# Attention with a mixture of experts on one core: where TensorE turns the inner layer of a tile, and which tests stand around it

## The chip, the core and the metric

The kernel runs on one core of a Trainium2 chip, as one launch. The metric is device time in microseconds (us). Three runs of the kernel before took 515.75 to 516.62 us, with a median of 516.23 us. Five engines work side by side, each with its own queue of instructions: TensorE (PE in the profile; its weight loads are listed apart as PEld), VectorE (DVE), ScalarE (ACT), GpSimd (POOL) and SyncE (SP, which starts most transfers). They wait for each other through semaphores: counters that an instruction raises when it is done, and on which another engine waits for a number.

## The reference

What is computed is causal attention followed by a mixture of experts in which every token goes to one expert:

```python
# q, k, v: (4, 12, 448, 64)
scores = q @ k^T / 8, masked above the diagonal
x = softmax(scores) @ v, laid out as (1792 tokens, 768)
# 8 experts, w1: (8, 768, 1024), w2: (8, 1024, 768)
logits = (x / |x|) @ (emb / |emb|)^T / tau
expert_idx = argmax(logits); gate_w = softmax(logits)[expert_idx]
for e in range(8):
    h = maximum(x[mask] @ w1[e], 0)
    out[mask] = gate_w[mask] * (h @ w2[e])
```

## The kernel before, in words

The first 220 us or so are the attention, whose order is written out by hand in a table; the change does not touch it. Then come the experts. Tokens are sorted by expert on the chip and cut into tiles of up to 128 tokens, each of one expert. With the inputs of the runs there are 18 tiles, numbered t = 0 to 17. Expert 4, the one with most tokens, comes first (tiles 0 to 4); the others follow in the order of their numbers.

Each tile has two matrix products. The first (`product1`, 768 to 1024) runs over 6 blocks of 128 rows of w1; its sums are copied to a tile `hb[t]`, the inner layer. The inner layer must be turned (transposed) before the second product (`product2`, 1024 to 768), which runs over 8 blocks of 128 rows of w2. To keep precision, numbers are split into a high and a low part (h and l): a block takes 6 matmuls (high by high, high by low, low by high, for two halves of the width). ACT casts the high part of a weight and DVE subtracts to get the low part; this is `split_w`, done only where a tile's expert is new.

Three kinds of tiles are told apart by a number that is computed on the chip and read into a register of each engine (`few[t]`):

- 1, a small tile: at most 64 tokens. High and low lie side by side in one operand, and a block takes 4 matmuls.
- 2, a light tile: over 64 tokens, and of the same expert as the tile before, so that no weights have to be split. Its inner layer is turned by DVE (16 transposes of 32 columns, `turn_light`), and TensorE turns nothing.
- 0: over 64 tokens, and of a new expert. TensorE turns the inner layer with 8 transposes (`turn_h`).

Tiles 2, 3, 7, 10, 13, 14 and 15 are light, tiles 4, 5, 8 and 17 are small, and tiles 6, 9, 11, 12 and 16 are neither. Tile 1 is treated as a whole tile without a test. A new expert begins at tiles 5, 6, 9, 11, 12, 16 and 17.

The loop `body(t)` writes out the work of the tile in flight. On TensorE the order is: first product of tile t, turn of the input rows of tile t+1 (`turn_x`), the first 7 blocks of the second product of tile t-1, the turn of the inner layer of tile t, and the last block of the second product of tile t-1. On ACT and DVE it is: split w1 for tile t+1 if its expert is new, copy the inner layer of tile t (`hiddens`), split the input of tile t+1 (`next_x`), DVE's turn if tile t is light, split the first 6 blocks of w2 for tile t if its expert is new, split the turned inner layer (`split_h`), scale and store tile t-1 (`finish`), split the last two blocks of w2. After the last tile there is no further first product: `last` runs its second product and stores it.

Since the tiles' kinds are known only on the chip, each choice is a test and a jump in every engine's queue (`either` and `branch`). All arms of such a choice must raise an engine's semaphore by the same amount by the place where they meet, so an arm in which an engine has nothing to do gets one instruction that waits for the engine's own earlier work and then raises the count (on TensorE line 577 of the helper `branch`). From tile 14 on the body stands inside a test on the number of tiles (`rest`, line 974), whose other arm, with the call of `last`, lies far behind in the program.

Of the kernel before, what the change touches and what calls it, by code (L numbers as in the profile page):

```python
# [16 lines left out]
ET = mybir.EngineType  # L17

P = 128
# [106 lines left out]
def attn_moe(tc, qk, vv, emb, tau, w1, w2, out):  # L126
# [3 lines left out]
    with ExitStack() as ctx:  # L130
# [10 lines left out]
        def cut(a, parts, *dims, at=0):  # L141

            n = 1
            for d in dims:
                n *= d
            a = a[:parts, at : at + n]
            if len(dims) == 1:
                return a
            names = "abcd"[: len(dims)]
            return a.rearrange(f"p ({' '.join(names)}) -> p {' '.join(names)}", **dict(zip(names, dims)))  # L150
# [3 lines left out]
        sp_ring, pt_ring = Ring(bank[0:2], bank[2:4]), Ring(*bank[4:6])  # L154
# [60 lines left out]
        def part(tile_, i, j, *dims):  # L215

            def f():
                t, n = tile_(), 1
                for d in dims:
                    n *= d  # L220
                return cut(t, P, *dims, at=i * DM + (j or 0) * F)
            return f
# [8 lines left out]
        th_ring = Ring(part(rr, 1, 0, KF, P), part(or_, 1, 0, KF, P))  # L231
        tl_ring = Ring(part(qr, 5, 0, KF, P), part(pr, 9, 0, KF, P))
# [325 lines left out]
        xs, hs, hb = {}, {}, {}  # L558
# [11 lines left out]
        def load_few(t, engines):  # L570
            return nc.values_load(small[0:1, t : t + 1], engines=engines, min_val=0, max_val=2,
                                  skip_runtime_bounds_check_because="made on chip within these bounds")

        def branch(flag, small_, whole_, light_=None):

            def rest():
                with tc.If(flag > 1) as c:
                    light_()
                with c.Else():
                    whole_()  # L580
            with tc.If(flag == 1) as c:
                small_()
            with c.Else():
                rest() if light_ else whole_()

        def either(t, engine, small_, whole_, light_=None):

            if t < 2:
                whole_()
            else:  # L590
                branch(few[t][engine], small_, whole_, light_)
# [21 lines left out]
        pf = {}  # L613

        def turn_x(t):
            xs[t] = (xs[t], xh_ring.next(), xl_ring.next())
            px = [cut(pt_ring.next(), P, 3, P) for a in range(2)]
            for a, pt in enumerate(px):
                for k in range(3):
                    pe.transpose(pt[:, k], xs[t][0][:, (3 * a + k) * P : (3 * a + k + 1) * P], idt)  # L620
            return px
# [2 lines left out]

        def turn_h(t):

            pf[t] = [cut(pt_ring.next(), P, 4, P) for a in range(2)]
            hs[t] = (hb[t], th_ring.next(), tl_ring.next())

            def rows(n):  # L630
                for k in range(KF):
                    pe.transpose(pf[t][k // 4][:, k % 4, 0:n], hb[t][0:n, k * P : k * P + P], idt[0:n, 0:n])
            either(t, ET.PE, lambda: rows(64), lambda: rows(P), lambda: None)

        def turn_light(t):

# [35 lines left out]
        def product(acc, xh, xl, wh, wl, ks, ends, w):  # L672

            for k in ks:
                for j in range(2):
                    o = slice(w * j, w * j + w)
                    pe.matmul(acc[j], xh[:, k], wh[k][:, o], start=k == ends[0], stop=False)  # L677
                    pe.matmul(acc[j], xh[:, k], wl[k][:, o], start=False, stop=False)  # L678
                    pe.matmul(acc[j], xl[:, k], wh[k][:, o], start=False, stop=k == ends[1])  # L679

        def small_product(acc, x, wh, wl, ks, nk, w):

            for k in ks:
                for j in range(2):
                    o = slice(w * j, w * j + w)
                    pe.matmul(acc[j], x[:, k], wh[k][:, o], start=k == 0, stop=False)
                    pe.matmul(acc[j], x[:, k], wl[k][:, o], start=False, stop=k == nk - 1)

        few = [None] * NT

        def product1(t, acc):
            either(t, ET.PE, lambda: small_product(acc, xs[t][1], h1, l1, range(KD), KD, 512),
                   lambda: product(acc, *xs[t][1:], h1, l1, range(KD), (0, KD - 1), 512))

        def product2(t, acc, ks=range(KF)):
            either(t, ET.PE, lambda: small_product(acc, hs[t][1], h2, l2, ks, KF, 384),
                   lambda: product(acc, *hs[t][1:], h2, l2, ks, (K0[0], K0[-1]) if t == 0 else (0, KF - 1), 384))

        def hidden(t, acc, j):
            if t not in hb:  # L700
                hs[t] = hb[t] = hh_ring.next()
            ac.copy(hb[t][:, 512 * j : 512 * j + 512], acc[j])  # L702

        def hiddens(t, acc):

            hs[t] = hb[t] = hh_ring.next()

            def low(j):
                return hb[t][0:64, 512 * j : 512 * j + 512]

            either(t, ET.Activation, lambda: [ac.copy(low(j), acc[j][64:128]) for j in range(2)],
                   lambda: [hidden(t, acc, j) for j in range(2)])
            either(t, ET.DVE, lambda: [v.tensor_tensor(low(j), acc[j][0:64], low(j), op=ALU.add) for j in range(2)],
                   lambda: v.memset(apart, 0.0))

        acc2 = [bo[:, :384], bx[:, :384]]
# [123 lines left out]
        pt_ring = Ring(*bank[2:6])  # L840
# [7 lines left out]
        def loads(t, which):  # L848
            if t >= NT:
                return  # L850
            if ee[t] is None:
                ee[t] = val(t, E - 1, [ET.SP])
                cc[t] = val(NT + t, 1, [ET.SP, ET.Activation, ET.DVE, ET.Pool])
            load(*((r1, w1, KD) if which == 1 else (r2, w2, KF)), ee[t], cc[t] != 0)

        def split_w(r, h, l, ks):
            for k in ks:
                ac.copy(h[k], r[:, k])  # L858
                v.tensor_tensor(l[k], r[:, k], h[k], op=ALU.subtract)  # L859

        def body(t):
            product1(t, acc1)
            if t == 1:
                halves()
            if t == 2:
                upper()
            elif t == 1:
                hidden(t, acc1, 0)
                hidden(t, acc1, 1)
            if t + 1 < NT:  # L870
                with tc.If(cc[t + 1] != 0):
                    split_w(r1, h1, l1, range(KD))
                loads(t + 2, 1)
            if t > 1:
                hiddens(t, acc1)
            if t + 1 < NT:
                few[t + 1] = {e: load_few(t + 1, [e]) for e in (ET.PE, ET.DVE, ET.Activation)}
            if t + 1 < NT:
                next_x(t + 1, turn_x(t + 1))
            if t + 3 < NT:  # L880
                gather(t + 3)
            if t == 1:
                gates()
            turn_light(t)
            ks = K0[GE:] if t == 1 else list(range(KF))
            product2(t - 1, acc2, ks[:-1])
            turn_h(t)
            product2(t - 1, acc2, ks[-1:])
            if t > 1:
                with tc.If(cc[t] != 0):  # L890
                    split_w(r2, h2, l2, range(6))
            split_h(t)
            finish(t - 1, acc2, False)
            if t > 1:
                with tc.If(cc[t] != 0):  # L895
                    split_w(r2, h2, l2, range(6, KF))
            loads(t + 1, 2)
# [35 lines left out]
        def halves():  # L933

            v.tensor_scalar(sm, us, 1.0 / SKIP, None, ALU.mult)
            f = pt_ring.next()[:, :NT]
            pe.matmul(f, idt[:, 64:65].broadcast_to([P, P]), sm, start=True, stop=True)
            same, t2 = T("same", [NT], parts=1), T("t2", [NT], parts=1)
            v.memset(same, 0.0)
            v.tensor_tensor(same[:, 1:], ef[:, 1:NT], ef[:, 0 : NT - 1], op=ALU.is_equal)  # L940
            v.tensor_tensor(t2, f[0:1], same, op=ALU.mult)
            v.tensor_tensor(same, same, t2, op=ALU.subtract)
            v.scalar_tensor_tensor(small, same, 2.0, f[0:1], op0=ALU.mult, op1=ALU.add)

        def upper():

            f = pt_ring.next()[:, :NT]
            pe.matmul(f[64:128], idt[:, 0:64], gt, start=True, stop=True, tile_position=(0, 64), skip_group_check=True)
            v.tensor_copy(gu[64:128], f[64:128])
# [67 lines left out]
```

## Time and profile before

| | |
|---|---|
| median of three runs | 516.23 us |
| the profiled execution | 516.48 us, of which the span of the instructions is 514.7 us |
| mean granted TensorE clock over the span | 0.992 |
| TensorE busy | 490.8 us (95% of the span) |
| VectorE busy | 348.4 us (68%) |
| ScalarE busy | 338.2 us (66%) |

The busy shares are means over attention and experts. The matmuls are pipelined, so that the time one is listed with (0.33 us) overlaps with the next: what counts is the distance between two starts, 0.17 us for a matmul of 384 columns. "PEq" is TensorE's sequencer, which reads the instructions, waits for semaphores and takes the jumps; it runs ahead of the matmuls.

### The profile page before, as it was taken

What the parts mean: (1) busy time and instruction counts of PE and PEld (TensorE: products, weight loads), DVE (VectorE), ACT (ScalarE), POOL (GpSimd) and SP (SyncE); (2) the same over time, 40 slices, a digit from 0 to 9 for tenths busy, and PEclk for the clock granted to TensorE, in tenths of its full rate; (3) what the DMA queues carried; (4) which work ended last, traced back from release to release, by engine and by line L of the source; (5) the groups of instructions that cost most, each with busy time, mean ns of one, the idle gap of its engine ahead of it and who ended that gap; (6) DMA issues with size and microseconds to landing.
All of it is one profiled execution on the core that took longest, in us unless ns stands there. A gap on an engine that the chain in (4) does not pass through costs nothing. (4 is left out here: it accounts for less than half of the span.)

```text
span 514.7 us, 10584 instructions
## 1 busy us (share of the span) xinstructions
PE 490.8 (95%) x3120; PEld 391.2 (76%) x3120; DVE 348.4 (68%) x945; ACT 338.2 (66%) x813; POOL 81.1 (16%) x90
## 2 busy tenths in 40 slices
PE   8999999999999978999999999999999999999983
PEld 5566566665666646889889898899989988898983
DVE  4776576586668659554486986846988454788871
ACT  5999999999999997231245963617566531256770
POOL 2000000000000560330111122200721020011101
PEclk9999999999999999899999999999999999999998
DMA  8223443263345960311349684368587312567831
GB/s 250 71 95 108 123 148 108 73 197 109 108 124 179 330 215 18 93 33 62 134 176 379 243 279 158 152 231 355 195 294 283 130 63 69 241 212 289 284 130 34
DMA packets 27368, 87.19 MB, mean 169 GB/s; under 512 B 2694, under 2 KB 3142, under 8 KB 27280
## 3 DMA queue, kind: packets, MB, share of 16 engines
q1 hardware_dynamic: 24160, 72.38, 40.8%
q0 software_dynamic: 3120, 13.77, 7.5%
q8 instruction: 39, 0.64, 0.5%
q14 instruction: 49, 0.40, 0.2%
HBM read 144.33 MB, written 12.58 MB: 305 GB/s over the span
## 5 line engine op out<-in xcount | busy, mean ns | idle before, releaser
L378 ACT ACTIVATE aq<-aq,mx 112x112 f32<-112x112 f32 (+3 forms) x192 | 99.8, 524 | 4.2 <-DVE mx L373 4.2
L373 DVE CUSTOM_DVE_ANT_0 aq<-bank,ar 112x112 f32<-112x112 f32 (+1 forms) x192 | 76.1, 442 | 30.0 <-PE bank L368 29.7
L396 PE MATMUL bank<-idt,aq 112*112 112x112 f32 x480 | 62.6, 265 | 1.6 <-ACT ap L401 0.8
L396 PEld LDWEIGHTS bank<-idt,aq 112*112 112x112 f32 x480 | 46.8, 133 | 19.8 <-ACT ap L401 7.0
L743 POOL DMA_INDIRECT out_dram<-fa,isx x18 | 32.5, 1803 | 179.4 <-DVEq L895 42.7
L368 PE MATMUL bank<-ak 64*112 64x112 f32 (+3 forms) x384 | 56.2, 416 | 0.9 <-DVE mx L373 0.8
L401 ACT COPY ap<-bank 112x336 f32<-112x336 f32 (+2 forms) x120 | 51.3, 459 | 2.9 <-PE bank L396 1.1
L409 PE MATMUL bank<-ap 112*64 112x448 f32 (+3 forms) x384 | 51.2, 406 | 1.1 <-ACT ap L401 1.1
L859 DVE TENSOR_TENSOR wl<-fa,wh 128x1024 fp32r<-128x1024 f32 x42 | 48.4, 1220 | 4.5 <-PE bank L678 2.7
L702 ACT COPY fa<-bank 128x512 f32<-128x512 f32 x28 | 15.2, 588 | 54.0 <-PE bank L677 49.3
L642 DVE STREAM_TRANSPOSE turned<-fa 32x256 f32<-32x256 f32 x112 | 48.8, 435 | 1.5
L409 PEld LDWEIGHTS bank<-ap 112*64 112x64 f32 x384 | 25.1, 136 | 31.6 <-issue 17.7
L858 ACT CAST wh<-fa 128x1024 fp32r<-128x1024 f32 x42 | 40.7, 1048 | 5.6 <-PE bank L679 3.1
L562 POOL DMA_INDIRECT fa<-xd,ig x21 | 24.0, 1144 | 84.8 <-PE bank L620 56.6
L378 ACT ACTIVATION_READ_ACCUMULATOR aq<-aq,mx 112x1 f32 x192 | 36.9, 192 | 0.0
L368 PEld LDWEIGHTS bank<-ak 64*112 64x112 f32 x384 | 27.0, 173 | 12.9 <-issue 3.1
L679 PE MATMUL bank<-wh,akr 128*128 128x512 f32 x84 | 32.9, 392 | 1.3 <-DVE akr L601 1.3
L677 PE MATMUL bank<-wh,aor 128*128 128x512 f32 x84 | 32.8, 391 | 0.2 <-ACT aor L600 0.2
L677 PE MATMUL bank<-wh,akr 128*128 128x512 f32 x84 | 33.0, 393 | 0.0
L679 PE MATMUL bank<-wh,apr 128*128 128x512 f32 x84 | 32.9, 392 | 0.0
L678 PE MATMUL bank<-wl,aor 128*128 128x512 f32 x84 | 32.8, 391 | 0.0
L678 PE MATMUL bank<-wl,akr 128*128 128x512 f32 x84 | 32.8, 390 | 0.0
(291 smaller groups left out, 1060.7 us busy)
## 6 DMA issues: line engine op xcount, KB each, us to landing
fa<-in_w_dram SPq DMA_DIRECT2D x76, 768.0 KB
fa<-in_w_dram SPq DMA_DIRECT2D x54, 1024.0 KB
ak<-in_qk_dram SPq DMA_DIRECT2D x24, 448.0 KB
ap<-in_vv_dram SPq DMA_DIRECT2D x24, 224.0 KB
xd<-fa SPq DMA_DIRECT2D x3, 1344.0 KB
fa<-in_w_dram SPq DMA_DIRECT2D x6, 512.0 KB
xd<-fa SPq DMA_DIRECT2D x1, 1120.0 KB
fa<-xd,ig POOLq DMA_INDIRECT x21, 5.7
```

Source lines behind the costliest of these rows:

```text
L368: pe.matmul(o, raws[p % 4][rows, 0, CP * i : CP * i + CP], raws[p % 4][rows, 1, :n], start=True, stop=True, tile_position=(D * h, 0), skip ...
L373: v.tensor_tensor_reduce(out=Ps[p % 2][i, h], in0=st.pop(("sp", p, i, h)), in1=mask[i], scale=-0.125, scalar=3e38, op0=ALU.add, op1=ALU.mi ...
L378: ac.activation(x, x, AF.Exp, bias=mxs[p % 3][:, h, i : i + 1], scale=-1.0, accum_out=sums[p % 3][:, h, i : i + 1])
L396: pe.transpose(t[:, x, c], Ps[p % 2][i, h][:, c * CP : c * CP + CP], idt[:CP, :CP])
L401: (ac.copy if q == "A" else v.tensor_copy)(o, st.pop(("pt", p, n)))
L409: pe.matmul(bo[64 * h : 64 * h + 64, CP * c : S], vts[p % 4][:, c, 64 * h : 64 * h + 64], PTs[p % 2][:, h, 4 * c : 3 * c + NC], start=c == ...
L642: v.transpose(xk[32 * j : 32 * j + 32, :, q : q + 32], blocks[q : q + 32, :, j])
L677: pe.matmul(acc[j], xh[:, k], wh[k][:, o], start=k == ends[0], stop=False)
L678: pe.matmul(acc[j], xh[:, k], wl[k][:, o], start=False, stop=False)
L679: pe.matmul(acc[j], xl[:, k], wh[k][:, o], start=False, stop=k == ends[1])
L858: ac.copy(h[k], r[:, k])
L859: v.tensor_tensor(l[k], r[:, k], h[k], op=ALU.subtract)
```

## The change

```diff
         def turn_h(t):
-            pf[t] = [cut(pt_ring.next(), P, 4, P) for a in range(2)]
-            hs[t] = (hb[t], th_ring.next(), tl_ring.next())
-
             def rows(n):
                 for k in range(KF):
                     pe.transpose(pf[t][k // 4][:, k % 4, 0:n], hb[t][0:n, k * P : k * P + P], idt[0:n, 0:n])
-            either(t, ET.PE, lambda: rows(64), lambda: rows(P), lambda: None)
+            either(t, ET.PE, lambda: rows(64), lambda: rows(P))
...
+        def turned_h(t, acc, ks):
+            pf[t] = [cut(pt_ring.next(), P, 4, P) for a in range(2)]
+            hs[t] = (hb[t], th_ring.next(), tl_ring.next())
+
+            n = 3 if t > 1 else 1
+
+            def among():
+                product2(t - 1, acc, ks[:-n])
+                turn_h(t)
+                product2(t - 1, acc, ks[-n:])
+            if t < 2:
+                among()
+            else:
+                with tc.If(few[t][ET.PE] > 1) as c:
+                    product2(t - 1, acc, ks)
+                with c.Else():
+                    among()
...
             ks = K0[GE:] if t == 1 else list(range(KF))
-            product2(t - 1, acc2, ks[:-1])
-            turn_h(t)
-            product2(t - 1, acc2, ks[-1:])
+            turned_h(t, acc2, ks)
```

Where tile t is light, TensorE now runs the whole second product of tile t-1 in one arm, with no test between its blocks. Where it is not, the product is cut after its fifth block instead of its seventh, and the turn stands there. The matmuls and transposes that are executed are the same ones. The program of TensorE gets longer, since the second product is written out in both arms.

TensorE's queue, second product of tile 3 around its last block (bank 72 and 73 are its two accumulators, 69 and 70 the turned layer; "waits PE_49" is a wait for TensorE's own count), before:

```order
L679 MATMUL bank_73<-apr 128x384
L581 UNCONDITIONAL_BRANCH
L871 UNCONDITIONAL_BRANCH
L581 UNCONDITIONAL_BRANCH x2
L581 COMPARE_AND_BRANCH
...
L581 UNCONDITIONAL_BRANCH
L577 COMPARE_AND_BRANCH
L577 UNCONDITIONAL_BRANCH [waits PE_49]
...
L581 COMPARE_AND_BRANCH
L686 MATMUL bank_72<-apr,aor 128x384 [waits Activation_49]
```

and after, the end of the light tile's arm (lines 674 to 676 are the former 677 to 679):

```order
L674 MATMUL bank_73<-apr,aor 128x384
L675 MATMUL bank_73<-apr,aor 128x384
L676 MATMUL bank_73<-apr 128x384
L674 MATMUL bank_72<-apr,aor 128x384 [waits Activation_49]
L675 MATMUL bank_72<-apr,aor 128x384 [waits DVE_49]
L676 MATMUL bank_72<-apr 128x384
L674 MATMUL bank_73<-apr,aor 128x384
L675 MATMUL bank_73<-apr,aor 128x384
L676 MATMUL bank_73<-apr 128x384
L581 UNCONDITIONAL_BRANCH
```

The seventh and the eighth block now follow each other, and the wait for TensorE's own count with its two tests is gone from between them; behind the arm stands one jump over the arm for the other tiles.

TensorE's queue in the other arm, after the fifth block of the same product (line 629 is the former 632, the transposes):

```order
L674 MATMUL bank_73<-apr,aor 128x384
L675 MATMUL bank_73<-apr,aor 128x384
L676 MATMUL bank_73<-apr 128x384
L581 UNCONDITIONAL_BRANCH
L581 COMPARE_AND_BRANCH
L629 MATMUL bank_69<-idt,fa 128x64 [waits DVE_49,Activation_49]
L629 MATMUL bank_69<-idt,fa 128x64 x3
L629 MATMUL bank_70<-idt,fa 128x64 [waits DVE_49,Activation_49]
L629 MATMUL bank_70<-idt,fa 128x64 x3
```

The transposes, which stood behind the seventh block, stand behind the fifth, with the same waits for DVE and ACT; three blocks of the product follow them.

## Rows read from the trace of the kernel before

**Rows 1.** The page: TensorE's busy time, and its granted clock in 40 slices.

```profile
PE 490.8 (95%) x3120; PEld 391.2 (76%) x3120; DVE 348.4 (68%) x945; ACT 338.2 (66%) x813; POOL 81.1 (16%) x90
PEclk9999999999999999899999999999999999999998
```

**Rows 2.** Waits of TensorE from 235 to 515 us: total, times, longest.

```profile
PE bank L677 <- PEq L577: 4.6, 7, 0.7
PE bank L686 <- DVE fa L735: 1.3, 1, 1.3
```

**Rows 3.** Line 577 from 235 to 515 us: duration ns min/median/max, first to last start.

```profile
L577 PEldq COMPARE_BRANCH  x19: 77/169/215, 242.5 to 479.5; - x19
L577 PEldq EVENT_SEMAPHORE  x7: 51/51/51, 245.6 to 464.3; - x7
```

**Rows 4.** Timeline, TensorE, light tile 10: start us, us, line, [idle before <-releaser].

```profile
372.77 0.33 PE L679 MATMUL bank<-apr 128*128 128x384 f32 x1
...
373.29 0.34 PE L679 MATMUL bank<-apr 128*128 128x384 f32 x1
374.32 0.44 PE L677 MATMUL bank<-apr,aor 128*128 128x384 f32 x1 [0.69 <-PEq L577]
374.61 0.34 PE L678 MATMUL bank<-apr,aor 128*128 128x384 f32 x1
```

**Rows 5.** Timeline, TensorE, light tile 2, the first.

```profile
245.18 0.34 PE L679 MATMUL bank<-apr 128*128 128x384 f32 x1
245.94 0.44 PE L677 MATMUL bank<-apr,aor 128*128 128x384 f32 x1 [0.42 <-PEq L577]
246.22 0.33 PE L678 MATMUL bank<-apr,aor 128*128 128x384 f32 x1
```

**Rows 6.** Timeline, TensorE, tile 11, whose inner layer TensorE turns.

```profile
391.47 0.34 PE L679 MATMUL bank<-apr,aqr 128*128 128x384 f32 x1
391.64 1.03 PE L632 MATMUL bank<-idt,fa 128*128 128x128 f32 x8
392.43 0.42 PE L677 MATMUL bank<-apr,arr 128*128 128x384 f32 x1
```

**Rows 7.** Timeline, TensorE, tile 5: its turn within the small tile 4.

```profile
291.46 0.34 PE L687 MATMUL bank<-apr,arr 128*128 128x384 f32 x1
291.73 0.71 PE L632 MATMUL bank<-idt,fa 64*128 64x64 f32 x8
```

**Rows 8.** Timeline, DVE: what those two turns wait for (tile 5, then tile 11).

```profile
289.50 1.27 DVE L713 TENSOR_TENSOR fa<-bank,fa 64x512 f32<-64x512 f32 x2
...
387.60 0.06 DVE L714 MEMSET apart<- 1x1 f32 x1
```

**Rows 9.** Busy time by stretch: us, then busy us of each engine.

```profile
235.00:375.00 140.00, 137.52 (x740) 123.97 (x739) 100.11 (x162) 71.11 (x108) 28.35 (x17) 1.00 0.60 220
```

**Rows 10.** Timeline, TensorE, second products of tiles 16 and 17.

```profile
490.29 0.42 PE L677 MATMUL bank<-arr 128*128 128x384 f32 x1
...
493.15 0.33 PE L678 MATMUL bank<-aqr,arr 128*128 128x384 f32 x1
...
499.40 0.34 PE L679 MATMUL bank<-apr,aqr 128*128 128x384 f32 x1
501.09 0.41 PE L686 MATMUL bank<-arr,aor 128*128 128x384 f32 x1 [1.35 <-DVE fa L735]
```

**Rows 11.** Timeline, ACT, the first cast of w2 for tile 17.

```profile
493.52 0.84 ACT L858 CAST arr<-fa 128x768 fp32r<-128x768 f32 x1 [1.75 <-PE bank L678]
```

**Rows 12.** Timeline, DVE: first low part of w2 and the turned layer of tile 17.

```profile
494.40 0.96 DVE L859 TENSOR_TENSOR aqr<-fa,arr 128x768 fp32r<-128x768 f32 x1 [2.23 <-ACT arr L858]
...
499.62 0.75 DVE L666 SCALAR_TENSOR_TENSOR aor<-bank,aor 128x256 fp32r<-128x256 f32 x2
```

**Rows 13.** Line 974 from 490 to 503 us: TensorE's jump to the last product.

```profile
L974 PEldq COMPARE_BRANCH  x1: 3797/3797/3797, 497.0 to 497.0; - x1
```

## The prediction

> **What bounds the kernel now.** [...] Then the waits of TensorE over the stretch of the experts. They come to two entries only: seven waits on its own sequencer, released at line 577, together 4.6 us, and one of 1.3 us before the very last product [rows 2]. Everything else in this stretch is matmuls end to end. So time is won by taking idle time out of TensorE's queue, and lost by putting some in; DVE and ACT matter where TensorE comes to wait for them.
>
> Line 577 is the arm of the light tiles in which TensorE has nothing to turn. It is taken seven times [rows 3], once for each light tile. The sequencer reads the test long before it matters: the first test is at 242.5 us, and the wait that follows it ends at 245.6 us [rows 3], so that the sequencer stands 3.1 us ahead of the matmuls. Then it waits there until TensorE's own matmuls are done, and loses its lead: in tile 10 the last matmul of the seventh block starts at 373.29 and the next one at 374.32 us [rows 4]. Where TensorE turns the layer itself, the same tests cost it nothing: matmul, transposes and matmul follow each other at 391.47, 391.64 and 392.43 us [rows 6].
>
> **The change part by part.**
>
> *The second product in one piece, seven times.* Matmuls of this product start 0.173 us apart (three steps from 372.77 to 373.29) [rows 4]. The first start after the gap is 1.03 us late instead of 0.173, and the one behind it comes 0.29 us after that instead of 0.173 (374.32 to 374.61): 0.97 us lost. The first light tile loses less, 0.76 and 0.28 instead of 0.173 each, so 0.69 us [rows 5]. The tests and the wait between the blocks go in the new arm, and no wait of another engine stood between these blocks to take their place. Gain: 6 x 0.97 + 0.69 = 6.5 us, all of it on the path, since TensorE is what bounds. One jump at the arm's end comes in; the sequencer's lead of 3.1 us hides it as it hides those around the transposes.
>
> *The test in the other tiles' body.* The test for a light tile moves from inside the turn to ahead of the product. Small tiles have one test more. At a median of 169 ns a test [rows 3] and with 3.1 us of lead: nothing. If the lead were gone, 4 x 0.17 us.
>
> *The turn two blocks earlier, in nine tiles (4, 5, 6, 8, 9, 11, 12, 16, 17).* The transposes are the same. They now need the inner layer 2 x 6 x 0.173 = 2.08 us earlier, or 2 x 4 x 0.173 = 1.39 us where the tile before is small. Two places come close. At tile 5 DVE's second half of the layer is done at 290.77 us [rows 8], and the transposes start at 291.73 [rows 7], their second half about 0.3 us later; 1.39 us earlier, that half would start at 290.64 and waits 0.1 to 0.2 us. If DVE did not follow the 1.66 us that tiles 2 and 3 have won by then, it would be 1.8 us. I take 0.15, as DVE adds up sums that come from TensorE and so moves with it. At tile 11 the turn waits for a memset by which DVE closes its branch (387.60 us [rows 8], the turn at 391.64 [rows 6]): 3.98 us of room. Off that go 2.08 for the earlier place, 1.73 for the late release described next (at tile 9, behind which DVE has a light tile's transposes and then weights to split), and 0.97 of tile 10, which DVE does not follow while it works without a break. That is 0.8 us too much at worst, nothing at best; I take 0.4. What the earlier turn gives ACT and DVE is nothing here: where the expert is new, both have six blocks of w2 to split ahead of the turned layer, and where it is not, `finish` still has to wait for the product's end.
>
> *A release that comes later.* This is not in the diff. A cast of a block of w2 for a new expert overwrites the block that the second product of the tile before reads; it waits for a count of TensorE. All arms must reach equal counts, and in the built program the count for the first cast is reached at the third matmul of the fifth block, where before it was the fifth matmul of the third: 10 matmuls or 1.73 us later (whole tile before; for a small one about as much or somewhat more). That this wait binds is seen at the end: matmul number 17 of the product that begins at 490.29 starts at 493.15 and runs 0.33 us [rows 10], and the cast starts at 493.52, released by that line [rows 11]. Six of the seven new experts have the first product of the next tile between this and the use of the weights, which hides it. Tile 17 has none: its second product comes right behind. DVE's chain there runs from the cast (493.52) over the first low part (494.40) and six of them to the turned layer at 499.62, of which the first half is done about 0.42 us later, at 500.04 [rows 11, 12]. Before, TensorE had to wait longer than that: until 501.09 [rows 10], because its sequencer was in the jump of line 974 from 497.0 for 3.80 us, that is until 500.8 [rows 13]. Counted from the product's start, DVE is now ready at 500.04 - 490.29 + 1.73 = 11.48 us, and the last product can start at some 11.6; before it started at 10.80. Cost 0.8 us. Bounds: 1.73, if the profile's releaser (DVE's scaling at line 735, which comes behind the turned layer) is the true one; -0.5, if DVE's chain doesn't move and the jump is read 0.5 us earlier (3.1 us ahead of the end instead of 499.57 - 497.0 = 2.6).
>
> *Sum.* -6.5 + 0.15 + 0.4 + 0.8 = -5.2 us against the profiled execution's 516.48 us: 511.3. The median of the runs shown is 0.25 us below that execution, so 511.0 us. With the costs at their least: -6.5 - 0.5, so 509.2; at their most (1.8, 0.8 and 1.73): -2.2, so 514.0.
>
> **The rivals.**
>
> *The skipped code has to be fetched (slower).* Every tile now jumps over an arm of up to 96 matmuls, where the largest arm skipped inside the body before had 36. The one long jump on the path took the sequencer 3.80 us [rows 13]. If every skip cost as much, it would exceed the lead of 3.1 us by 0.7 us in 16 bodies: 11 us, so 522 us. It decides from the point where a skip takes over 3.1 us. For it speaks that line 974 is the same kind of instruction; against it, that this jump goes past whole bodies of tiles and that each of the seven light arms and nine others skips far less than one body.
> [...]
>
> *The gain is handed back in waits (no change).* If DVE and ACT stand still in time instead of following TensorE, for instance because weights land no sooner, each turned tile waits for its layer: nine times 0.6 us and the tail's 1.73 use up the 6.5 us: 516 us. For it: tile 5 has under 1 us of room. Against: DVE is busy for 100.1 of 140 us in this stretch [rows 9], and no wait of TensorE for DVE, ACT or a transfer appears before the tail [rows 2].
>
> *The idle time moves instead of going (less faster).* If the sequencer doesn't get its lead back by the arm's end, the jump there costs part of what the wait cost; with half of it left, 3.3 us return: 514.3 us. Against it: the tests around the transposes, which come as thickly, cost nothing [rows 6].
>
> **How the numbers follow.** The forecast has a chance of 0.76, the fetched code 0.07, the handed-back gain 0.08, the idle time that moves 0.09. Differences of up to 0.2% (1.03 us) can't be told from no change in this kernel. So faster: 0.76 + 0.09 = 0.85; within 0.2%: 0.08; slower: 0.07. The range goes from 509.2, the least costs, to 514.3, which takes in the greatest costs and the third rival.
>
> **What would show it.** In the profile after, the seven waits for the sequencer are gone from TensorE's list, and starts in a light tile are 0.17 us apart through all eight blocks. Turns at tiles 5 and 11 show waits of under 1 us. The first cast of w2 for tile 17 comes about 5.0 us after the start of tile 16's second product, instead of 3.2, and the last product starts 11.6 us after it instead of 10.8. I am wrong if gaps stand in front of first products or turns (fetching), if TensorE waits for DVE in most turned tiles, or if the last product starts no later than before.

## The result: slower, and the profile after

The changed kernel takes 520.48 us (median of four runs, 520.44 to 521.60) against 515.99 us for the kernel before on the same chip (four runs, 515.67 to 516.62): a ratio of 1.0087, 95% interval 1.0075 to 1.0099. It is slower by 4.5 us, where 511.0 us was forecast. The range (509.2 to 514.3) doesn't hold the time, and the case that came true is the rival "the skipped code has to be fetched", which had a chance of 0.07. The ratios in this document leave out two executions that took far longer than the others of the same kernel: one of 2199 us in the first run of experiment 4, and one of 702 us of the kernel before.

The profiled execution has a span of 518.7 us, 4.0 more than before. First the page, the answer to [rows 1]:

```profile
PE 491.9 (95%) x3120; PEld 392.6 (76%) x3120; DVE 348.3 (67%) x945; ACT 337.8 (65%) x813; POOL 81.2 (16%) x90
PEclk9999999999999999999999999999999999999997
```

The instructions are the same in number. TensorE is busy for 1.1 us more than before and idle for 2.9 us more, so most of the 4.0 us are idle time; the other part is matmuls that took longer, and is read below. Its waits from 235 to 520 us (total, times, longest) answer to [rows 2]:

```profile
PE bank L675 <- issue: 2.8, 1, 2.8
PE bank L683 <- DVE aor L663: 2.2, 1, 2.2
PE bank L674 <- issue: 1.4, 2, 0.9
PE bank L674 <- DVE fa L730: 0.5, 1, 0.5
PE bank L674 <- DVE turned L639: 0.3, 1, 0.3
```

The seven waits for line 577 are gone. New are waits of lines 674 and 675 for "issue", which means that the profile shows nothing the engine waited for. Line 581 is a test on TensorE's sequencer (PEldq); its row over the experts (duration in ns min/median/max) has the same median as the kernel before's, 205, but that one's longest was 338:

```profile
L581 PEldq COMPARE_BRANCH  x69: 63/205/3800, 243.5 to 501.8; - x69
```

Now light tile 10, the answer to [rows 4], with what stands behind it:

```profile
372.18 0.33 PE L675 MATMUL bank<-apr,aor 128*128 128x384 f32 x1
372.35 0.34 PE L676 MATMUL bank<-apr 128*128 128x384 f32 x1
373.63 0.47 PE L674 MATMUL bank<-wh,aor 128*128 128x512 f32 x1 [0.94 <-issue]
```

Inside the arm the matmuls start 0.17 us apart to the end, as forecast; the 0.97 us are won. But the next product starts 1.28 us after the last matmul of this one instead of about 0.2. The sequencer has two records ahead of it. By the order of the program the first (0.18 us) is the jump at the arm's end, and the second, the 3.80 us of the row above, is the test ahead of tile 11's first product, which itself skips only some 50 instructions:

```profile
L581 PEldq COMPARE_BRANCH  x2: 179/1990/3800, 369.4 to 369.7; - x2
```

So the wait is recorded on the test behind the long jump, not on the jump. The sequencer stood in that test from 369.67 to 373.47 us, longer than its lead of 2.7 us (372.35 minus 369.67). Within it the instruction queue q8 moved one block of code; over the whole span it moved 49 (0.80 MB, so 16 KB a block), where before it was 39 (0.64 MB). The DMA view from 371.0 to 372.2 us (packets, MB, share of the stretch):

```profile
q8 instruction: 1, 0.02, 5.1%
```

There are five places where TensorE stands still: ahead of the first products of tiles 11 (1.15 us more than before), 14 (0.49) and 15 (0.72), ahead of the second product of tile 16 (0.76), and, the largest, inside the first product of tile 16:

```profile
462.65 0.40 PE L674 MATMUL bank<-wh,akr 128*128 128x512 f32 x1
465.88 0.79 PE L675 MATMUL bank<-wl,akr 128*128 128x512 f32 x1 [2.83 <-issue]
466.47 0.63 PE L676 MATMUL bank<-wh,akr 128*128 128x512 f32 x1
466.89 0.63 PE L674 MATMUL bank<-wh,akr 128*128 128x512 f32 x1
```

Four of the five stand behind the arm of a light tile (10, 13, 14 and 15). The one at tile 16's second product stands in the body of tile 17, which is not light: there the test that skips the light arm's 166 instructions took 0.22 us and the next test 3.59 us. Behind the arms of tiles 14 and 15 no test took over 0.31 us; what TensorE waited for at tile 15 and inside tile 16's first product is thus not seen on a test. But inside the last of these gaps the instruction queue moved a block as well (the DMA view from 463.3 to 464.6 us):

```profile
q8 instruction: 1, 0.02, 4.8%
```

Not every long test costs something: the one of line 711 (the test for a light tile) at 327.25 us took 2.46 us, but the last matmul ahead of it started at 330.52 us, so that the sequencer had a lead of 3.3 us there, and no gap stands behind it.

At the last of the five places TensorE had one matmul of this product, then nothing for 2.83 us, and after that matmuls stood 0.42 us apart instead of 0.23. The stretches show why (the seventh figure, before the DMA share, is the granted clock):

```profile
462.00:466.00 4.00, 1.17 (x7) 0.79 (x5) 3.10 (x8) 0.71 (x1) 0.00 (x0) 0.94 0.43 173
466.00:469.00 3.00, 3.00 (x7) 2.35 (x8) 1.75 (x2) 0.82 (x2) 0.00 (x0) 0.51 0.87 267
469.00:475.00 6.00, 6.00 (x28) 4.94 (x27) 3.05 (x3) 4.13 (x5) 1.02 (x1) 1.00 1.00 365
```

After the idle time the clock stood at 0.51 for about 3 us. This place costs 4.55 us in all, and the five together 7.7 us.

The end, the answers to [rows 10 to 12]; first TensorE, then ACT, DVE and POOL:

```profile
492.10 0.41 PE L674 MATMUL bank<-arr 128*128 128x384 f32 x1 [0.51 <-DVE fa L730]
...
503.74 0.41 PE L683 MATMUL bank<-arr,aor 128*128 128x384 f32 x1 [2.18 <-DVE aor L663]
```

```profile
497.08 0.83 ACT L875 CAST arr<-fa 128x768 fp32r<-128x768 f32 x1 [4.56 <-PE bank L676]
```

```profile
503.16 0.76 DVE L663 SCALAR_TENSOR_TENSOR aor<-bank,aor 128x256 fp32r<-128x256 f32 x2
...
511.55 1.13 DVE L746 SCALAR_TENSOR_TENSOR fa<-bank,gt,fa 64x384 f32<-64x384 f32 x2 [5.37 <-DMA out_dram<-fa,isx]
```

```profile
505.25 1.82 POOL L760 DMA_INDIRECT out_dram<-fa,isx  x1 [12.41 <-DVE fa L752]
```

The first cast for tile 17 comes 497.08 - 492.10 = 4.98 us after the start of tile 16's second product (before 3.23, forecast 5.0), and the last product 503.74 - 492.10 = 11.64 us after it (before 10.80, forecast 11.6). What the forecast missed stands behind that: the last scaling (line 746) writes the same buffer that tile 16's store reads, and waits for the store to land. The kernel before had that store issued 0.61 us after the last product's start, and its last scaling, at 507.41 us, waited for ACT, not for a store:

```profile
501.70 1.02 POOL L743 DMA_INDIRECT out_dram<-fa,isx  x1 [9.93 <-ACT apr L858]
```

```profile
507.41 1.13 DVE L729 SCALAR_TENSOR_TENSOR fa<-bank,gt,fa 64x384 f32<-64x384 f32 x2 [4.72 <-ACT fa L726]
```

Now it is issued 1.51 us after it and takes 0.8 us longer to issue: 1.35 us more between the last product's start and the end.

The sum by places: -6.5 in the light tiles, +0.7 at turns (those of tiles 4, 5 and 8), +7.7 at the five places, +0.8 and +1.35 at the end, together +4.05, against a difference of 4.0 us between the spans.

### The profile page after: what moved, and what is told of

Same layout as the page of the kernel before. It is cut to its first block, busy times and chain, and to the rows that moved or that the text cites. A ratio compares the mean times of both kernels' runs of the same rounds, so it can differ in the third digit from the quotient of the medians.

```text
span 518.7 us, 10565 instructions
## 1 busy us (share of the span) xinstructions
PE 491.9 (95%) x3120; PEld 392.6 (76%) x3120; DVE 348.3 (67%) x945; ACT 337.8 (65%) x813; POOL 81.2 (16%) x90
```

## Experiments

Theory A says that the loss comes from TensorE's code: the long arms make it skip 166 instructions in nine tiles, 208 in six and some 137 in tile 2 (a matmul with its weight load counts as two), where no skip inside a body was longer than 99 before, and at some of these skips the sequencer waits until code has been brought. Theory B blames the order of the work: the earlier turn, the later release, and what ACT and DVE do then. Each result is the median, the ratio to the kernel before on the same chip, and its 95% interval.

**1. The turn back in its place, the arms as long as in the changed kernel.**

```diff
-            n = 3 if t > 1 else 1
+            n = 1
```

> The changed kernel, but the turn of the other tiles stands one block ahead of the end again (n = 1). The arms, and so the skips of 166 to 208 instructions, stay as long as in the changed kernel. Theory A (long skips make TensorE's sequencer wait for code, about 7.7 us in the changed kernel's trace; the early turn costs 0.7 us): 518 to 521 us, and tests of 2.5 to 4 us on the sequencer as in the changed kernel. Theory B (the time went into the earlier turn and what ACT and DVE do then): the early turn's cost is gone, 510 to 513 us.

Measured: 520.20 us, ratio 1.0062 (1.0041 to 1.0083). Nothing is won back by the median; four of the six executions took 520.17 to 520.72 us, the other two, which were not profiled, 517.58 and 518.20. The stalls stand at the same five places, with the same test of 3.83 us at most, and the same one inside tile 16's first product:

```profile
PE bank L675 <- issue: 2.8, 1, 2.8
PE bank L683 <- DVE aor L663: 2.2, 1, 2.2
PE bank L674 <- issue: 0.9, 2, 0.5
PE bank L674 <- ACT akr L647: 0.8, 1, 0.8
PE bank L674 <- DVEq L905: 0.4, 1, 0.4
```

The early turn is not the cause. The end is that of the changed kernel too: the last product starts 11.61 us after tile 16's second product, so the later release comes with the long arms and not with the place of the turn. Two of these stalls are put down to ACT and DVE here. The same two stand under DVE in the changed kernel's list, and both have a long test ahead of them (3.83 and 3.02 us), so their cause is taken to be the code too.

**2. The early turn alone.** The kernel before, with

```diff
+            n = 3 if t > 1 else 1
-            product2(t - 1, acc2, ks[:-1])
+            product2(t - 1, acc2, ks[:-n])
             turn_h(t)
-            product2(t - 1, acc2, ks[-1:])
+            product2(t - 1, acc2, ks[-n:])
```

> The kernel before, with only the place of the turn moved from one to three blocks ahead of the end; the light tiles keep their two pieces, the test and the wait between them (now three blocks ahead of the end). No skip is longer than 99 instructions. Theory A: the seven gaps of about 0.7 to 1 us stay, the turns at three tiles wait 0.7 us in all, no test takes over 1 us ahead of the last jump: 516 to 517.5 us. Theory B: 519 us or more.

Measured: 517.76 us, 1.0029 (1.0017 to 1.0041). The seven waits for line 577 stay (4.8 us in all), and no test ahead of the last jump is longer than 0.42 us. The early turn costs 1.6 us by itself, a little more than expected, and the turns have the smaller part of it. ACT shows where it is lost, in the casts of w2 for tile 17 (line 858 is the cast):

```profile
495.32 0.83 ACT L858 CAST apr<-fa 128x768 fp32r<-128x768 f32 x1
497.75 0.84 ACT L858 CAST apr<-fa 128x768 fp32r<-128x768 f32 x1 [1.59 <-PE bank L679]
```

The last of the six casts ahead of the turned layer waits 1.59 us for TensorE; before it did not wait (496.47, two casts end to end). The whole chain to the store is later by that, and from the last product's start to the end of the span it takes 15.9 us instead of 13.6.

**3. Short arms.** Seven blocks ahead of the test, and only the turn and the last block inside the arms:

```diff
-            def among():
-                product2(t - 1, acc, ks[:-n])
...
+            n = 1
+            product2(t - 1, acc, ks[:-n])
...
                 with tc.If(few[t][ET.PE] > 1) as c:
-                    product2(t - 1, acc, ks)
+                    product(acc, *hs[t - 1][1:], h2, l2, ks[-n:], (0, KF - 1), 384)
                 with c.Else():
-                    among()
+                    turn_h(t)
+                    product2(t - 1, acc, ks[-n:])
```

The light arm can call `product` at once, since the tile before a light one is never small.

> Seven blocks of the second product stand ahead of the test; only the turn and the last block stand in the two arms, so that the light tile's arm holds a block of matmuls and no wait for TensorE's own count, and no skip is longer than 99 instructions. The turn stands one block ahead of the end. Theory A: the seven gaps go (6.5 us) and no code is waited for: 509 to 510.5 us. Theory B says the same here, as the turn is not moved; if it is instead the missing wait that does harm (TensorE's lead no longer held back), 515 us or more.

Measured: 508.77 us, 0.9857 (0.9843 to 0.9871): 7.4 us faster than before, and 0.2 us under the range expected. This is the fastest kernel of the study. TensorE has one wait left in the stretch of the experts, and no long test ahead of the jump to the last product:

```profile
PE bank L683 <- ACT apr L873: 1.1, 1, 1.1
```

```profile
L581 PEldq COMPARE_BRANCH  x64: 63/206/393, 242.8 to 496.1; - x64
```

So the gaps of the light tiles were a real gain of about the size forecast (of the 7.6 us between the profiles 0.7 stand ahead of the experts, where the two kernels do the same), and no time is lost by the missing wait.

**4 and 7. Short arms with a long skip.** A third arm that is never taken, with 96 transposes and a block of matmuls, beside the two of kernel 3:

```diff
+                with tc.If(few[t][ET.PE] > 2) as d:
+                    for k in range(96):
+                        pe.transpose(pf[t][k // 4 % 2][:, k % 4], idt, idt)
+                    product(acc, *hs[t - 1][1:], h2, l2, ks[-n:], (0, KF - 1), 384)
+                with d.Else():
+                    end()
```

> The kernel with short arms, with one more arm beside them that is never taken (a third value of the tile's kind, which does not occur) and holds 96 transposes and a block of matmuls: 16 bodies now skip 206 instructions in the order in which they skipped under 100. What is executed is that of the kernel with short arms, and one test more a tile. Theory A: the skip by itself brings the stalls back, 3 to 10 us over the kernel with short arms, with tests of 2.5 to 4 us on TensorE's sequencer and more code transfers. Any theory in which the order of the work, the early turn or the late release made the loss: the same as with short arms within 1 us.

> The kernel with the long skip (206 instructions, 16 times) once more, for a trace of an execution of usual length. By the median so far 529.6 us. Theory A: TensorE's sequencer shows tests of 2.5 to 4 us at the lines of the new arm in most of the 16 bodies, each with an idle gap of TensorE behind it, about 20 us in all, and the instruction queue moves more blocks while a gap lasts. Rival C: the gaps stand behind tests of usual length (0.2 us).

Measured: 529.59 us, 1.0253 (1.0234 to 1.0272), and again 529.08 us, 1.0232 (1.0212 to 1.0253). The trace read here is that of the second run, an execution of 533.02 us, 3.9 us above its median. Code that never runs costs about 20 us, twice the upper figure expected. In the trace six of the 16 bodies show a gap of 1.6 to 3.1 us, 12.2 us together, fewer and longer than "most of the 16 bodies". Each stands behind a test of 3.4 to 5.8 us. Two of them, with the two lines of tests:

```profile
381.55 0.47 PE L674 MATMUL bank<-wh,aor 128*128 128x512 f32 x1 [2.29 <-issue]
```

```profile
476.26 0.76 PE L674 MATMUL bank<-wh,akr 128*128 128x512 f32 x1 [3.07 <-DVEq L911]
```

```profile
L581 PEldq COMPARE_BRANCH  x64: 63/207/4542, 243.4 to 520.3; - x64
L706 PEldq COMPARE_BRANCH  x23: 70/188/5752, 242.5 to 507.9; - x23
```

Much of the rest is the granted clock, which fell behind three of the gaps: its mean was 0.83 from 290 to 300 us, 0.81 from 451 to 460 and 0.74 from 472 to 485, together 6.8 us of the full clock at most. With the 12.2 us of gaps that is 19.0 of the 22.4 us by which this span (531.3 us) is longer than that of the control in experiment 5 (508.9); what is left is not taken apart.

**5. The control: the third arm without its transposes.**

> The control to the kernel with the long skip: the same third arm that is never taken, and so the same extra test a tile, but the arm holds only the block of matmuls and none of the 96 transposes; no skip inside a body is longer than 99 instructions. Theory A (the loss comes from code that is skipped and must be waited for): as with short arms, 508 to 510 us, the extra test being hidden by the sequencer's lead. Rival C (the extra test or the third arm itself makes the loss of 20.8 us): 525 us or more.

Measured: 509.87 us, 0.9872 (0.9857 to 0.9887). The test and the arm cost about 1 us (kernel 3 had 508.77); rival C falls.

**6 and 11. 48 and 72 transposes in it.**

> The same third arm with 48 transposes instead of 96: 16 skips of 110 instructions instead of 206. Theory A with a cost that grows with the length of the skip, counted from the length that costs nothing (99 instructions at most in the kernel with short arms): 510 to 513 us. Theory A with a cost per skip that does not depend on its length: 525 to 530 us. Rival C: 525 us or more, and the same in the control.

> The kernel with short arms and the third arm that is never taken, with 72 transposes in it: 16 skips of 158 instructions, between the 110 that cost 1.4 us over the control and the 206 that cost 19 us. A cost that begins at some length and then grows evenly (from 110 to 206: 0.18 us an instruction) gives 520 us; a cost that jumps where a skip comes near the length of a block of code leaves it at 511 to 514 us.

Measured: 511.28 us, 0.9907 (0.9891 to 0.9923), and 512.50 us, 0.9925 (0.9908 to 0.9942). With skips of 110 one body of 16 shows a gap (1.3 us), with 158 three do, and with 206 six:

```profile
355.10 0.47 PE L674 MATMUL bank<-wh,akr 128*128 128x512 f32 x1 [1.30 <-DVE apr L882]
```

```profile
290.56 0.68 PE L629 MATMUL bank<-idt,fa 64*128 64x64 f32 x8 [1.17 <-ACT aqr L881]
...
307.72 1.06 PE L629 MATMUL bank<-idt,fa 128*128 128x128 f32 x8 [1.83 <-DVE apr L882]
...
356.36 1.06 PE L629 MATMUL bank<-idt,fa 128*128 128x128 f32 x8 [0.54 <-ACT apr L881]
```

Over the control that is 1.4, 2.6 and 19.2 us. The cost does not rise evenly: from 158 to 206 it rises by 16.6 us, so that the even growth (520 us at 158) is out. But each of these arms also moves all the code behind it, which experiments 9, 10 and 12 show to matter by itself. So the three runs show that skips of 110 to 206 instructions can cost time; how the cost depends on the length alone they don't show. All three are shorter than a block, which by an estimate holds 256 instructions: with 0, 48, 72 and 96 transposes in the third arm, of two instructions each and in 16 bodies, queue q8 moved 41, 47, 50 and 53 blocks, 12 more for 3072 instructions more. The estimate takes it that the code of every arm is brought, run or not.

**8. Short arms with the early turn.** Kernel 3 with `n = 3 if t > 1 else 1`.

> The kernel with short arms, with the turn three blocks ahead of the end: five blocks of the second product ahead of the test, and the arms hold three blocks. Skips inside a body are 103 instructions at most (six times). The releases of the weight blocks come no later than with the turn one block ahead. Theory A: the early turn alone costs what it cost in the kernel that had only that (1.5 us), so 509 to 511 us, with three turns that wait for 0.7 us in all and no long test. Theory B (early turn makes the loss once the wait of the light tiles is gone): 513 us or more.

Measured: 511.69 us, 0.9905 (0.9890 to 0.9920), 2.9 us over kernel 3 and 0.7 over the range expected. 0.7 us of the profiled difference stands ahead of the experts, where the two kernels do the same. Behind the last product's start it has 15.3 us instead of 13.5, and the sixth cast waits for TensorE as in experiment 2:

```profile
492.53 0.84 ACT L873 CAST apr<-fa 128x768 fp32r<-128x768 f32 x1 [1.59 <-PE bank L676]
```

Theory B as the cause of the loss (513 us or more) falls; the early turn is a small loss with either arms. That no release would come later did not hold for this cast, which with kernel 3 follows the one before it without a wait.

**9, 10 and 12. The changed kernel, its code moved.** At tile 2 alone a third arm that is never taken puts what follows 98, 194 or 256 instructions later in TensorE's program (m is 0, 48 or 79):

```diff
+            elif t == 2:
+                with tc.If(few[t][ET.PE] > 2) as d:
+                    for k in range(m):
+                        pe.transpose(pf[t][k // 4 % 2][:, k % 4], idt, idt)
+                    product2(t - 1, acc, ks)
+                with d.Else():
+                    kinds()
```

`kinds` is the changed kernel's choice of arms.

> The changed kernel; at tile 2 alone one arm more that is never taken and holds a second product, so that everything behind it on TensorE stands 98 instructions later in the program. What is executed is the same, and one test more. Open is why only 5 of the 15 long skips of the changed kernel cost TensorE idle time. Theory D (it depends on where a skip begins and ends in the blocks of code that the instruction queue brings, 16 KB each): the stalls stand at other tiles than 11, 14, 15, 16 and 17, and the sum differs from 7.7 us by some us: 515 to 525 us. Theory E (it depends on what the kernel does there, the queues being busy with weights at those tiles): stalls at the same places, 520 to 522 us.

> The same with 48 transposes more in the arm that is never taken, so that everything behind it stands 194 instructions later (with a first skip of 194 at tile 2). Theory D: yet other places and another sum, 513 to 526 us. Theory E: the same places as in the changed kernel, 520 to 522 us.

> [...] Theory D in its full form (only the place within a block decides): the stalls are back at tiles 11, 14, 15, 16 and 17, with the drop of the clock in the first product of tile 16: 519 to 523 us. If the place within a block doesn't matter and any longer program helps (as the two before, 98 and 194 later, might also be read): 512 to 516 us, without stalls at these tiles.

Measured: 98 later 513.06 us, 0.9939 (0.9926 to 0.9953); 194 later 514.44 us, 0.9966 (0.9953 to 0.9979); 256 later 520.33 us, 1.0093 (1.0073 to 1.0114). The waits of TensorE with the code 98 later, in which hardly any stall is left:

```profile
PE bank L683 <- DVE aor L663: 2.2, 1, 2.2
PE bank L629 <- DVE apart L739: 0.7, 1, 0.7
PE bank L674 <- issue: 0.4, 2, 0.2
```

And 256 later:

```profile
PE bank L675 <- issue: 2.8, 1, 2.8
PE bank L683 <- DVE aor L663: 2.2, 1, 2.2
PE bank L674 <- issue: 1.5, 2, 0.9
PE bank L674 <- DVE fa L740: 1.1, 1, 1.1
PE bank L674 <- ACT aor L647: 0.6, 1, 0.6
PE bank L674 <- DVE turned L639: 0.3, 1, 0.3
```

The two records ahead of tile 11's first product (the jump at the arm's end, then the test), 98 later and then 256 later:

```profile
L581 PEldq COMPARE_BRANCH  x2: 212/252/293, 369.2 to 369.6; - x2
```

```profile
L581 PEldq COMPARE_BRANCH  x2: 176/1932/3688, 369.6 to 369.8; - x2
```

Moved by 256 instructions, one block by the estimate above, the kernel has its stalls back at the same five places (tests of 3.69, 2.86 and 4.10 us where the changed kernel has 3.80, 2.88 and 3.59); moved by 98 it has none of them, and moved by 194 three others of 0.8 to 1.2 us idle (where the trace is that of the slowest of six executions, 516.72 us). Theory D had still put 98 later at 515 to 525 us, with stalls at other places; there were next to none, and the time lies 2 us under that. The instruction queue moves 49, 50 and 50 blocks: the number of blocks is the same with and without stalls. So what theory D says in its full form, that the place within a block decides, agrees with the three runs, and E and "any longer program helps" fall; which places wait was not forecast. The drop of the clock did not come back: after the same idle time of 2.81 us the granted clock stayed at 1.00 (256 later, the stretch that stood at 0.51 in the changed kernel):

```profile
466.00:469.00 3.00, 2.86 (x13) 2.36 (x13) 1.75 (x2) 1.11 (x2) 0.00 (x0) 1.00 0.70 213
```

Tile 2's one skip of 256 costs 0.6 us in its place.

## Why the prediction was wrong

- **The light tiles' gain: right.** 6.5 us were won in the places and sizes given; with nothing else in the way (experiment 3) it is 7.4 us over the whole kernel.
- **The tests in the other bodies: right but for the code.** They cost nothing where no code is waited for (98 later: no test of over 0.42 us at line 581). In the changed kernel one of them has a share in the loss: the skip over the light arm ahead of tile 16's second product (0.76 us), which was put at nothing. The prediction also counted 36 matmuls in the largest arm skipped before; seven blocks of six are 42. Nothing hangs on that.
- **The jump at the arm's end: wrong, and this is the step that failed.** It was put as "One jump at the arm's end comes in; the sequencer's lead of 3.1 us hides it as it hides those around the transposes". Those around the transposes skip at most 99 instructions; this one 208. At the next test behind this jump the sequencer stood for 3.80 us (ahead of tile 11) and 2.88 us (ahead of tile 14), which its lead of 2.7 and 2.4 us at these places did not cover; at tiles 15 and 16 TensorE stood still behind the same jump without a long test. The price is read from two kernels that differ, but for one test at tile 2, in the place of their code alone: 520.48 - 513.06 = 7.4 us. The rival had the mechanism and its point of decision (a skip of over 3.1 us), but asked whether every skip costs as much (16 times 0.7 us). What decides, by experiments 9, 10 and 12 (513.06, 514.44 and 520.33 us for the same work), is where in the program the skips stand: few skips cost anything, the cost is not the same, and one place of 4.55 us outweighs the others.
- **The reason for the low chance** was the author's estimate that skips of this length cost nothing, which no run shows. Skips of 110, 158 and 208 instructions, all shorter than the 256 estimated for a block, each showed stalls: 1.3 us idle in one body, 3.5 us in three, and 7.7 us lost at the changed kernel's five places. What the runs show is that 256 instructions later the five stalls are back (520.33 us), 98 or 194 later they are not (513.06 and 514.44 us). That a skip might cost time in some places was the open point, and it should have carried a price.
- **The turn: right in kind, too small.** Without the stalls (98 later) the turns cost 2.0 us together instead of 0.55, counted from the matmul ahead of a turn to the second one behind it: 0.9 at tile 11, where the wait is the one named, for the memset that closes DVE's branch (0.7 us), 0.5 at tile 5 instead of 0.15, and 0.3 each at tiles 4 and 8, which were not named. In the changed kernel itself they cost 0.7 us and nothing at tile 11; that the stall of 1.15 us ahead of it gave DVE this time back is argued, not shown.
- **The later release: right in its place, too small in its price.** Cast and last product came at 4.98 and 11.64 us, as forecast (5.0 and 11.6). The term was 0.8 us because it ended at the last product's start. The chain goes on over the scaling and the store of tile 16, whose buffer the last scaling needs: another 1.35 us. With the 1.45 us more at the turns that is 2.8 us, against 2.1 us between the 511.0 us forecast and the 513.06 us without stalls; the trace of the latter reaches the experts 0.7 us earlier than that of the kernel before.
- **What stays open:** which offsets make a skip wait was not worked out, and the 2.83 us inside tile 16's first product have no long test ahead of them; they belong to the place of the code, as they come and go with it (2.81 us with the code 256 later, none with 98 later) and a block of code is moved within them.

## What to carry to other kernels

Count the instructions that a jump skips on each engine, before and after, as one counts the instructions that run: here code that is only skipped cost from 1.4 to about 20 us by its length and place, so keep what differs in the arms and leave the common work outside (kernel 3 wins the same idle time and keeps every skip inside a body under 100, without a long test). A kernel with long skips can lose its gain by a shift of its code that no one sees in the source; if waits for "issue" stand behind tests of some 3 us, move the code by some 100 instructions, once, to tell this cause from others: 98 later took 7.4 us off the changed kernel, while its wait of 2.2 us ahead of the last product stood at every offset. And follow a later release to the end of its chain: to the buffer that the last store holds, not to the next matmul.

## What the runs showed of the hardware that was not expected

- A test on TensorE's sequencer takes 0.2 us in the median, but 2.88 to 3.80 us ahead of three of the changed kernel's five idle places (at the other two no test took over 0.31 us) and up to 5.75 us (line 706) in experiment 7. Each of the changed kernel's three had one block of code moved within it, in 0.98, 0.91 and 0.98 us (5.1% of 16 DMA engines over 1.2 us, 5.7% and 6.1% over 1 us), so the wait is longer than the transfer. In the changed kernel the long record is that of the test behind a long skip (2.9 to 3.8 us), while the long skip's own record is 0.18 to 0.29 us.
- The same code at another offset takes 7.4 us less (520.48 and 513.06 us), and comes back to the same time and the same five places after a shift of 256 instructions (520.33 us).
- An idle time of 2.8 us on TensorE was followed by about 3 us at a granted clock of 0.51 in one execution (the changed kernel), and by a clock of 1.00 in another with the same idle time (its code 256 later).
